# Two recurrent attention layers and two FFNs on one core: the first and last weight loads in other pieces, and another written order

## The chip, the cores and the metric

One core of one Trainium2 chip. The metric is device time in microseconds, here the median of five runs. The engines are named as the profile names them: PE is TensorE (PEld its weight loads), DVE is VectorE, ACT is ScalarE, POOL is GpSimd, and SP is SyncE, which only issues DMAs. Each engine, SP too, takes its instructions strictly in program order; an instruction waits for semaphores of other engines or of landed DMAs.

## The reference

The input x is 2048 x 576 in bf16. Block A, a layer of attention with recurrent memory, is applied to layernorm(x) and added to x; block B, a gated FFN, is applied to the layernorm of that and added; then A and B once more, with the same weights.

Block A cuts the sequence into 64 segments of 32 rows. The output of a segment's first 8 rows is the memory of the next one:

```python
for s in range(n_seg):
    xs = x[:, s * seg_len:(s + 1) * seg_len, :].copy()
    h = jnp.concatenate([mem, xs], axis=1)          # 8 + 32 rows
    q = jnp.einsum('btd,dhe->bhte', h, Wq)          # 32 heads of 128; k and v alike
    scores = jnp.einsum('bhqe,bhke->bhqk', q, k) * scale
    scores = jnp.where(mask[None, None], scores, -1000000000.0)
    p = _softmax(scores, axis=-1)
    o = jnp.einsum('bhqk,bhke->bhqe', p, v)
    o = jnp.einsum('bhte,hed->btd', o, Wo)
    mem = o[:, :M, :].copy()
```

Block B is `einsum(silu(x w1) * (x w3), w2)` with a hidden width of 4608.

## The kernel before

**Steps.** The two attention layers run interleaved. Layer two is LAG = 8 segments behind layer one, so there are 72 steps; steps 8 to 63 treat one segment of each layer side by side (80 columns instead of 40), the first and last eight only one. Wq and Wk stay in SBUF in `W` (128 partitions x 9 x 4096: four chunks of 128 input rows for each of Wq and Wk, and the ninth for the remaining 64 rows, Wq's on partitions 0 to 63, Wk's on 64 to 127), Wv in `WV`, Wo in `WO`. The FFN weights do not fit beside them and are streamed again for each block of 128 rows, in 18 tiles ("prs") of 256 hidden columns, through two slots of `W13` (w1 and w3) and two of `W2C` (w2).

**Work of a step, and its letters.** PE's order is written out as a string with one letter for a group of matmuls: Q, eight units of query and key projections of four heads (32 matmuls), and q, their remainder over the last 64 rows (8); S the scores of eight heads; T the transposes of the softmaxed P; P the product with V; O and o the output projection and its remaining 64 columns; V, X, G and v, x, g the value projections and their remainders; F and f the FFN's up projections and remainder, W and w its down projection for layer one and two; m, a, b, p, n transposes around the layernorms. `plan` (line 76) walks PE's letters in the written order and gives the work of the other engines to ACT or DVE by priorities and modelled times; DMA issues go into SP's queue in the order in which the planner comes to them. What matters for PE besides the order is the tiling of its array, `mode` in `make_nodes`: "full" (128 x 128) for Q, T, P, O, F, W, G and the transposes; "row" (two tiles of 64 rows) for q, f, g; "col" (tiles of 64 columns) for S, o and wide V and X; "c32", "oct" and "quad" for the narrow V and X and their remainders.

**What sets the order.** A step begins with Q, which needs the memory rows that the step before wrote from its o (`y_mem`). Scores go over PSUM to DVE (mask add, maximum, subtraction), ACT (exp), DVE (sum, reciprocal, multiplication into `PB`), back to PE (T). All groups take their PSUM from eight banks; a bank is free when its last reader is done. The string is FIRST (16 steps), eleven times FOUR (4 steps), LAST (12 steps).

**First loads** (`load_qk`, line 642; `load_tail`, 649; `load_v`; `load_o`). The order on SP is one half of the remainders, Wq in four transfers of 1 MB, Wk likewise, WV in four, WO in eight pieces of four heads; ACT issues the other half of the remainders. Each unit of Q in step 0 waits for all of Wq and Wk (`ld_qk`). Ahead of the first Q stand 18 matmuls that compute nothing, six for each of three Wk chunks, each waiting for its chunk (`qk`, line 895). At most eight of these transfers are in flight: an issue waits for the one eight places before it.

**Last loads** (`job`, from line 464; `tail_load`, 694). The FFN of the last 128 rows runs when attention is over. Its first two tiles (pr 16 and 17) are kept in W13 and W2C from the FFN before; they are called the kept pair. The other 16 come in eight units of two tiles: units 0, 1 and most of 2 go into `WV`, the rest into `W`, whose space is free when all of the last step's Q are done. They are issued from SP.

**Heads.** Group g of eight heads holds heads 4g to 4g+3 and 16+4g to 16+4g+3 (`head`), and the blocks of `V` and the columns of WV are numbered to match.

Of the kernel before, what the change touches and what calls it, by code (L numbers as in the profile page):

```python
# [13 lines left out]
P = 128  # L14
R64 = 64
D = 576
# [168 lines left out]
def ewh(*ns):  # L185
# [4 lines left out]
FIRST = (  # L190
    "amQqqQSQqQqQQSqqqqQQSSxXVvTPTPOTOPooTOoPOoQQqqvqqSVQQQqSTQqqqQSQPXSxOTPTOPTOPoooOoQQqqqQqSQqSVqvQQqqSQQaTSPTOPTo"
    "PTOPOOoooVqqvQQQSqqQQqqSQQqSqTPQOTSPXoTOPToxPOOooQQpqqqQvSVqqQQnQSfqFQSqqQTFPfSTOFPfWTOPfFToOPFOoooWQqfqQQqfqSFv"
    "VQQSfqFQFqTfSPQqTWPQFffqOTSoxPOWXTFPOFOoooWQfqqQFSfqqQQvVqSTQFqfQQFPfSqqQWOoSTFPfFTOPWTOPooffOoFQQqqVSvWqQFQfqQS"
    "qTWQqqqQPSQTOPabOSXTXPTOPoooxOoxVvpQQqqqQQqnSSqqfQFQfFTSQqqfFPQOTSoWPFTffOPFTOPWOoooFQqqfQQQSqqfFGQqgqQTSSPQgqqO"
    "WGTQFPSofgGTFfGPOTgfFPOWOoooFQqfqQWFSqfqQQFqqfSQWQTvVQSfqFPQTqfOSPFTOPfWOTFPFOooooWQfqqQqqfSFQQWQaqqSQQbTQSqgqGS"
    "gPGTGPOTggGPOTOPoooOoQqqppQQQSqqqQnnvVSfqFQFTQPSqfqQFfSWTOPwFTffFPOTOPwOWffooooFQFqqQWwQQSqqQfqFFTSfgqQGwWFPfSQQ"
    "gqqGTGSgPOWTOPwfgGTFPOFOooooffFQQqqvVSqqQQWQqSwTQPFqqQTSffqFQwPOWTSffOPFFTOaPWwOooooFqfqQQWQSqqqQQSQbqqqQQTGgSgS"
    "PGTGPOTggGPOTwPOOoooo"
)
FOUR = (  # L200
    "QqqvpQQpQqqVnSSqQnQFfqfFTQqqSQPFffSTFOPwTWOPFTOPWOfooooFwQqqfQQqqSWQQqqgSQwTGFPSffFGQqgqQTOPFTSfggGGPOTOPWwOoooo"
    "FfqfFQwWFQqfqQQqfvVSSFFQfqqQWTawPFqfqSQQTWOwffoSFPFTOPwTOPWOoooFfqqQQWQqqSQQqqSbQQqqgGTQPSSgGTGPOggTGPOTwPOOoooo"
)
LAST = (
    "VvqqpQQpQqqSQQnSqQnQqqqQTFPSSffTFPOOwFToffPFTOWPFOoooffFQQqqqQWwQSfqqFQWGgqTQSPwFQfqFQTSqfgGGPOTSogOPWwFfgfFTGOP"
    "wWFOfoooFfqqQQWVSqqvQQwFTSfqQFPWwqfQFSqqfQQTwWPSOTFPFffTOPOOooooWQqqQQqqSvQQQqqSVSTQqqbPQTOPvSVXTwPOTOPxoooOoVpp"
    "vqQQqqQQSqnQnQSqqfFQFTqSfqPQOTFPSoffTOFPwTOPWOoooFQqqfQwWFfSvVqqQQFqfqQQWTwSSqQPQFffqFTwOPSWTFffFPOTOPWwOxooooXQ"
    "FqqfQQqfSVvFFfqQWwSFTQfqqQQPSqqTOPQOooSfTWwPFTFPOOooWQfqqQwSqqQQFSqqfQQvVTSWPOTQPQqqwSoTbOoXPTxPOOooQqqqpQQSvqqV"
    "QQnQSfqFSqTQfqPFQTOPSfFwOTFPToofPOOooFQfqqQQSqfqFvVQQQqqSTwPQSqfqQFOSoTFPwTOPfxXTFPOOooowQqfqQQSqfFqVvQQSqqQTQSq"
    "qfFPQOTSofPFOTwPFTOPooffOoFQQqqwSqqQQvqSVqQQwQSTqfFPqQTfSPFTOOPwTOPoooOfopFFnffFwFfffFFwFffwFFfFwffFFwffFFwffFFw"  # L210
    "ffFFwffFFfww"
)
# [10 lines left out]
def make_nodes(em, nseg, pools, o=Opt, dma_bw=230e3, load_bw=400e3):  # L223
# [4 lines left out]
    def node(*a, **k):  # L228
        n = Node(*a, **k)
        nodes.append(n)  # L230
        return n
# [18 lines left out]
    ld_m0 = node("ACT", 0.1, em.load_m0(), prio=-90, name="m0", lat=2.5)  # L250
    ld_t = [node("ACT", 0.2, em.load_tail(1), prio=-80, name="ldt", lat=8.0), load("ldt", kb(R64, 6144), -20, em.load_tail(0))]
    ld_qk = [load("ldqk", kb(512, 4096), kind - 9.0, em.load_qk(kind)) for kind in (0, 1)] + ld_t
    ld_v = [load("ldv", kb(512, 4096), -7.0, em.load_v())] + ld_t
    ld_o = [load("ldo", kb(1024, 576), g - 6.0, em.load_o(g)) for g in range(NG)]
# [45 lines left out]
    def v_nodes(name, t, k, prio, tail_at, emit, strips, deps, tail_deps, free):  # L300

        modes = ("col", "quad") if strips[0][3] == R64 else ("c32", "oct")
        b = banks()
        m_ = node("PE", 8 * 0.2158, emit(b, False), deps=deps, prio=prio, mode=modes[0], acq=b, name=name)
        n = node("PE", 0.2158, emit(b, True), deps=deps + tail_deps, prio=prio + tail_at, mode=modes[1], acq=b, name=name + "t")
        reads_ht.setdefault(t, []).extend([m_, n])
        for r in (0, 1):
            outs = em.v_parts(strips, r)
            b[r].users = len(outs)
            for p0, width, row, blk in outs:  # L310
                e = node("AD", ew(512), em.v_ev(b[r], p0, width, row, blk), deps=[m_, n] + free.get(blk % 4, []), prio=prio + 0.01 * (blk % 4),
                         rel=[b[r]], name=name + "e")
                vx_ev.setdefault((name, t, blk % 4), []).append(e)
        return [m_, n]
# [16 lines left out]
    def vg_out(t, g, b, deps, row):  # L331

        return [node("AD", ew(512), em.v_ev(b[r], row, R64, row, NG * r + g), deps=deps, prio=t + o.vm + 0.01 * g + (0.05 if row == 0 else 0.0), rel=[b[r]],
                     name="VGe") for r in (0, 1)]
# [10 lines left out]
    def step(t):  # L345
# [17 lines left out]
        for g in range(NG):  # L363
            qs, qe = [], []
            for u in (2 * g, 2 * g + 1):
                q = Slot("qkt", users=1)
                b = banks()
                pq = t + o.qk + o.ustep * u
                m_ = node("PE", 32 * mm80, em.qk(t, u, b), deps=hx + hm[:1] + (ld_qk if t == 0 else []),
                          prio=pq, mode="full", acq=[q] + b, name="QK")  # L370
                n = node("PE", 4 * mm80, em.qk_tail(t, u, b), deps=hx + hm + (ld_qk if t == 0 else []), prio=pq + o.qkt, mode="row",
                         acq=[q] + b, name="QKt")
# [72 lines left out]
    def job(j):  # L445
# [18 lines left out]
        if last:  # L464
            v_done, qk_done, wo_done = last_reads
            tail = []
            for i in range(8):
                if i == 2:
                    parts = [(0, 9 * 512, v_done), (1, 4 * 576, qk_done)]
                else:  # L470
                    parts = [(None, 9 * 512 + 4 * 576, v_done if i < 2 else qk_done + wo_done[max(i - 4, 0):i - 3])]
                tail.append([load("tail", kb(128, c), s0 + o.tail_at + 0.01 * i, em.tail_load(i, what), deps=dep) for what, c, dep in parts])
# [89 lines left out]
class Emitter:  # L562
# [78 lines left out]

    def load_qk(self, kind):
        def f(n):
            wd = (self.a.wq, self.a.wk)[kind]
            for c in range(4):
                self.dma(self.T.W[:, 4 * kind + c, :], wd[c * P:(c + 1) * P, :])
        return f

    def load_tail(self, r):

        def f(n):
            go, wd, rr = ((self.dma, self.a.wq), (self.adma, self.a.wk))[r] + (slice(r * R64, (r + 1) * R64),)
            go(self.T.W[rr, 8, :], wd[4 * P:D, :])
            go(self.wv(True)[rr, :], self.a.wv[4 * P:D, r * 2048:(r + 1) * 2048])
        return f
# [6 lines left out]
    def load_v(self):  # L662
        def f(n):
            for c in range(4):
                self.dma(self.wv(False)[:, c, :], self.a.wv[c * P:(c + 1) * P, :])
        return f

    def load_o(self, g):
        def f(n):
            for h0 in (4 * g, H // 2 + 4 * g):  # L670
                self.dma(self.T.WO[:, h0:h0 + 4, :], self.a.wo[h0:h0 + 4].rearrange("h e d -> e h d"))
        return f

# [20 lines left out]
    def tail_load(self, i, what):  # L694

        def f(n):
            T = self.T
            qk, wv = T.W[:].rearrange("p a b -> p (a b)"), T.WV[:]
            n13, n2 = 9 * 512, 4 * D
            k = n13 + n2  # L700
            if i < 2:
                t13, t2 = wv[:, i * k:i * k + n13], wv[:, i * k + n13:(i + 1) * k]
            elif i == 2:
                t13, t2 = wv[:, 2 * k:2 * k + n13], qk[:, 5 * k:5 * k + n2]
            else:
                t13, t2 = qk[:, (i - 3) * k:(i - 3) * k + n13], qk[:, (i - 3) * k + n13:(i - 2) * k]
            fa = i * 512
            t13 = t13.rearrange("p (c f) -> p c f", c=9)
            t2 = t2.rearrange("p (b d) -> p b d", b=4)
            if what != 1:  # L710
# [105 lines left out]
    def v_mm(self, t, b, strips, tail):  # L816
# [4 lines left out]
        for c in ((4,) if tail else range(4)):  # L821
            for r in (0, 1):
                for p0, c0, q, m, row in strips:
# [4 lines left out]
                    else:  # L828
                        w0 = (4 * r + q) * 512
                        self.mm(out, HTt[:, c, c0:c0 + m], W[:, c, w0:w0 + 512], first and c == 0, c == 3, tile_position=(0, p0))  # L830

    def vg(self, t, g, b, tail):

        def f(n):
# [4 lines left out]
            for c in ((4,) if tail else range(4)):  # L839
                for r in (0, 1):  # L840
# [3 lines left out]
                    else:  # L844
                        w0 = (4 * r + g) * 512
                        self.mm(self.bk(b[r])[:], HTt[:, c, 32:160], W[:, c, w0:w0 + 512], first and c == 0, c == 3)
# [6 lines left out]
    def narrow(self, c0, row):  # L853

        return [(64 * ab + 32 * i, c0, 2 * i + ab, 32, row) for ab in (0, 1) for i in (0, 1)]

# [8 lines left out]
    def v_parts(self, strips, r):  # L865

        return [(p0, m, row, 4 * r + q) for p0, _, q, m, row in strips]

# [14 lines left out]
    def head(self, g, j):  # L883

        return H // 2 * (j // 4) + 4 * g + j % 4

    def qk(self, t, u, b):

        def f(n):
            q0, q1 = self.qcols(t)  # L890
            HTt = self.ht(t)
            first = self.begin(b)
            for c in range(3 if t == u == 0 else 0):
                for _ in range(6):
                    self.mm(self.bk(b[1])[:], self.T.ident[:, 0:P], self.T.W[:, 4 + c, 0:512], True, True)
            for j in range(4):
# [423 lines left out]
```

## Time and profile before

| | |
|---|---|
| median of 5 runs | 2710.03 us (2707.76 to 2711.33) |
| profiled execution | 2710.07 us, span 2708.3 us, mean granted PE clock 0.997 |
| PE busy | 2646.2 us, 98% |
| DVE, ACT, POOL busy | 78%, 51%, 12% |
| HBM | read 308.49 MB, written 2.36 MB: 115 GB/s over the span |
| DMA queue q1 | 477,696 packets, 38.0% of 16 engines' span |

The page gives busy time by engine, the chain of work that ended last, and groups of instructions with the idle time before them and what ended it. A matmul's mean time is its latency; consecutive ones overlap, and how far apart they start is read from the trace's start times. The window view gives the same busy times for chosen stretches. The waits view names who waited for whom; the timeline gives instructions in order, equal neighbours merged, with start and length.

### The profile page before, as it was taken

Reading aid. Unit: us, or ns where it says so; the run is one execution under the profiler, and the core shown is the slowest. Engines: PE = TensorE matmul, PEld = TensorE weight load, DVE = VectorE, ACT = ScalarE, POOL = GpSimd, SP = SyncE. Lnnn points to the kernel's source line nnn. Section 1 sums busy time; section 2 is a strip of 40 time slices with the busy share of each in tenths; the row PEclk is TensorE's granted clock in tenths of the full one; section 3 lists DMA queues with packets and bytes.
Section 4 is the critical chain, followed back from the end, with each engine's and each line's share of the span. In section 5 each row is a group of like instructions: output and inputs, shape, how many; then the busy total and the mean of one; then the engine's idle time right before and its main releaser. Section 6 shows DMA issues by size and latency. Waiting matters only on the chain.

```text
span 2708.3 us, 126684 instructions
## 1 busy us (share of the span) xinstructions
PE 2646.2 (98%) x55801; PEld 2229.9 (82%) x55801; DVE 2105.5 (78%) x5431; ACT 1378.4 (51%) x3970; POOL 333.3 (12%) x400
## 2 busy tenths in 40 slices
PE   5999999999999999999999999999999999999998
PEld 3788888888888888888888888888888888888886
DVE  4778887887878788787878878787887878787876
ACT  2655554554545455454545545454554545354553
POOL 1111110110101011010101101010110101011110
PEclk8999999999999999999999999999999999999999
DMA  9064533334342433434233343423334342425358
GB/s 315 4 175 129 147 94 114 88 109 125 99 133 79 117 89 109 125 99 131 80 116 92 110 125 96 135 76 116 95 110 125 92 132 70 134 88 151 94 169 260
DMA packets 481593, 321.42 MB, mean 119 GB/s; under 512 B 26280, under 2 KB 476720, under 8 KB 479376
## 3 DMA queue, kind: packets, MB, share of 16 engines
q1 hardware_dynamic: 477696, 305.44, 38.0%
q8 instruction: 437, 7.16, 1.1%
q0 software_dynamic: 3024, 6.93, 0.9%
q10 hardware_dynamic: 320, 0.94, 0.1%
q14 instruction: 116, 0.95, 0.1%
HBM read 308.49 MB, written 2.36 MB: 115 GB/s over the span
## 4 chain that ended last, share of the span: by engine, by line
PE 90%; DVE 4%; DMA 3%; ACT 2%; issue 1%; SPq 0%; POOL 0%; ACTq 0%; DVEq 0%
PE bank L581 90%; DMA W<-in_B_w_dram 1%; DVE STAT L587 1%; ACT V L584 1%; DVE SME L587 1%; DVE HTT L587 1%; DMA W<-in_A_Wk_dram 1%; DVE PB L587 1%; DVE V L587 1%; DMA WV<-in_A_Wv_dram 0%; DMA W2C<-in_B_w_dram 0%; SPq L590 0%; DVE PTS L587 0%; ACT QKT L584 0%; ACT HT L584 0%
## 5 line engine op out<-in xcount | busy, mean ns | idle before, releaser
L581 PEld LDWEIGHTS <-W 128*128 128x128 bf16 (+1 forms) x29400 | 1226.6, 98 | 145.7 <-issue 50.2
L581 PE MATMUL bank<-HT,W 128*128 128x80 bf16 (+3 forms) x23040 | 811.0, 197 | 11.7 <-ACT HT L584 6.2
L581 PE MATMUL bank<-XTB,W 128*128 128x256 bf16 (+3 forms) x6360 | 651.2, 262 | 6.6 <-DMA W<-in_B_w_dram 5.8
L584 ACT ACTIVATE QKT<-bank 128x256 bf16<-128x256 f32 (+4 forms) x1555 | 366.5, 308 | 408.2 <-PE bank L581 394.2
L999 POOL MEMSET PB<- 128x1024 bf16 x288 | 274.1, 952 | 1802.4 <-PE bank L581 1502.2
L581 PE MATMUL bank<-OT,WO 128*128 128x80 bf16 (+2 forms) x11520 | 409.6, 198 | 1.7 <-DVE OT L587 0.7
L584 ACT ACTIVATE V<-bank 64x512 bf16<-64x512 f32 (+1 forms) x605 | 342.9, 587 | 122.6 <-PE bank L581 116.4
L581 PEld LDWEIGHTS <-WO 128*128 128x128 bf16 (+1 forms) x11520 | 380.4, 102 | 17.5 <-issue 8.9
L581 PE MATMUL bank<-WV,HT 128*32 128x512 bf16 (+4 forms) x3240 | 367.1, 383 | 1.9 <-ACT HT L584 1.3
L581 PE MATMUL bank<-W2C,HTT 128*128 128x288 bf16 x2240 | 315.7, 286 | 0.7 <-DMA W2C<-in_B_w_dram 0.6
L587 DVE TENSOR_REDUCE STAT<-SME 104x8 f32<-104x320 f32 (+1 forms) x576 | 275.2, 478 | 16.8 <-ACT SME L584 11.6
L587 DVE TENSOR_TENSOR PB<-SME,STAT 40x128 bf16<-40x128 f32 (+4 forms) x912 | 275.6, 336 | 13.5
L584 ACT ACTIVATE HTT<-bank 128x512 bf16<-128x512 f32 (+1 forms) x324 | 178.1, 550 | 189.6 <-PE bank L581 187.5
L587 DVE SCALAR_TENSOR_TENSOR HTT<-HTT,bank 128x512 bf16<-128x512 bf16 (+1 forms) x324 | 201.1, 621 | 78.4 <-ACT HTT L584 76.8
L581 PEld LDWEIGHTS <-HT 128*32 128x32 bf16 (+4 forms) x3240 | 138.5, 96 | 147.7 <-issue 24.2
L587 DVE SCALAR_TENSOR_TENSOR XR<-bank,XR 128x288 f32<-128x288 f32 x576 | 243.5, 448 | 9.7 <-PE bank L581 3.2
L581 PEld LDWEIGHTS <-HTT 128*128 128x128 bf16 x2304 | 210.0, 98 | 48.2 <-issue 0.8
L587 DVE TENSOR_TENSOR HTT<-HTT,bank 128x512 bf16<-128x512 bf16 (+1 forms) x324 | 203.6, 628 | 30.0 <-DVE HTT L587 1.4
L584 ACT ACTIVATE SME<-SME 104x320 f32<-104x320 f32 (+1 forms) x288 | 136.0, 472 | 175.4 <-DVE SME L587 172.0
L587 DVE CAST QKT<-bank 128x128 bf16<-128x128 f32 (+2 forms) x493 | 136.6, 318 | 107.9 <-PE bank L581 105.0
L584 ACT ACTIVATE OT<-bank 128x320 bf16<-128x320 f32 (+1 forms) x382 | 144.6, 406 | 141.0 <-PE bank L581 137.8
L587 DVE CAST V<-bank 64x512 bf16<-64x512 f32 (+1 forms) x259 | 177.1, 684 | 39.4 <-PE bank L581 34.1
(64 smaller groups left out, 1805.1 us busy)
## 6 DMA issues: line engine op xcount, KB each, us to landing
W<-in_B_w_dram SPq DMA_DIRECT2D x612, 256.0 KB, 3.4
W2C<-in_B_w_dram SPq DMA_DIRECT2D x306, 288.0 KB, 3.1
W<-in_B_w_dram SPq DMA_DIRECT2D x612, 32.0 KB, 3.1
W<-in_B_w_dram SPq DMA_DIRECT2D x10, 512.0 KB, 9.1
WO<-in_A_Wo_dram SPq DMA_DIRECT2D x8, 576.0 KB, 9.2
XR<-in_A_x_dram POOLq DMA_DIRECT2D x16, 288.0 KB, 2.9
W<-in_A_Wq_dram SPq DMA_DIRECT2D x4, 1024.0 KB, 14.8
W<-in_A_Wk_dram SPq DMA_DIRECT2D x4, 1024.0 KB, 17.1
```

The lines of the kernel that those rows point to most:

```text
L581: self.ch("PE", self.nc.tensor.matmul(out, lhsT=lhsT, rhs=rhs, start=start, stop=stop, skip_group_check=True, **k))
L584: self.ch("ACT", self.nc.scalar.activation(*a, **k))
L587: self.ch("DVE", getattr(self.nc.vector, fn_)(*a, **k))
L999: return lambda n: self.ch("POOL", self.nc.gpsimd.memset(self.T.PB[:, pb.i], 0.0))
```

## The change

1. Wq and Wk load by halves of the heads (columns 0 to 2047, then 2048 to 4095): for each half the four chunks of Wq, the four of Wk (512 KB each), then both remainders (256 KB each), all from SP. A unit of Q in step 0 waits only for its own half. WV's two remainders follow WV's four mains, on SP.
2. The groups hold eight consecutive heads, so WO loads in four transfers of eight heads. V's blocks and WV's columns are numbered anew to match.
3. There are 12 warming matmuls, three for each of four Wk chunks.
4. The last FFN's units load otherwise: unit i's w1 and w3 go into the 512 columns of `W` that the last step's Q unit i read, its w2 into `WV`. The first waits for that unit of Q, the second for the last V; units 4 to 7 also for an output projection.
5. FIRST, FOUR and LAST are new strings with the same number of each letter.

```diff
+    ld_h = [load("ldqk", kb(512 + 2 * R64, 4096), half - 9.0, em.load_qk(half)) for half in (0, 1)]
+    ld_v = [load("ldv", kb(512 + 2 * R64, 4096), -7.0, em.load_v())]
-                m_ = node("PE", 32 * mm80, em.qk(t, u, b), deps=hx + hm[:1] + (ld_qk if t == 0 else []),
+                m_ = node("PE", 32 * mm80, em.qk(t, u, b), deps=hx + hm[:1] + ([ld_h[u // 4]] if t == 0 else []),
...
             for i in range(8):
-                if i == 2:
-                    parts = [(0, 9 * 512, v_done), (1, 4 * 576, qk_done)]
-                else:
-                    parts = [(None, 9 * 512 + 4 * 576, v_done if i < 2 else qk_done + wo_done[max(i - 4, 0):i - 3])]
+                late = wo_done[i - 4:i - 3] if i >= 4 else []
+                parts = [(0, 9 * 512, qk_done[2 * i:2 * i + 2] + late), (1, 4 * 576, v_done + late)]
...
+    def load_qk(self, half):
+        def f(n):
+            h = slice(half * 2048, (half + 1) * 2048)
+            for kind, wd in ((0, self.a.wq), (1, self.a.wk)):
+                for c in range(4):
+                    self.dma(self.T.W[:, 4 * kind + c, h], wd[c * P:(c + 1) * P, h])
+            for kind, wd in ((0, self.a.wq), (1, self.a.wk)):
+                self.dma(self.T.W[kind * R64:(kind + 1) * R64, 8, h], wd[4 * P:D, h])
+        return f
...
+            for r in (0, 1):
+                self.dma(self.wv(True)[r * R64:(r + 1) * R64, :].rearrange("p (q n) -> p q n", q=NG),
+                         self.a.wv[4 * P:D, :].rearrange("p (q r n) -> r p q n", q=NG, r=2)[r])
...
-            for h0 in (4 * g, H // 2 + 4 * g):
-                self.dma(self.T.WO[:, h0:h0 + 4, :], self.a.wo[h0:h0 + 4].rearrange("h e d -> e h d"))
+        return lambda n: self.dma(self.T.WO[:, g * GH:(g + 1) * GH, :], self.a.wo[g * GH:(g + 1) * GH].rearrange("h e d -> e h d"))
...
+            t13, t2 = T.W[:, :, fa:fa + 512], T.WV[:, i * 4 * D:(i + 1) * 4 * D].rearrange("p (b d) -> p b d", b=4)
...
-        return H // 2 * (j // 4) + 4 * g + j % 4
+        return GH * g + j
...
-            for c in range(3 if t == u == 0 else 0):
-                for _ in range(6):
-                    self.mm(self.bk(b[1])[:], self.T.ident[:, 0:P], self.T.W[:, 4 + c, 0:512], True, True)
+            for c in range(4 if first and t == 0 and u % 4 == 0 else 0):
+                for _ in range(3):
+                    self.mm(self.bk(b[1])[:], self.T.ident[:, 0:P], self.T.W[:, 4 + c, u * 512:(u + 1) * 512], True, True)
```

FOUR, the part of the order that is repeated, before and after:

```diff
-    "QqqvpQQpQqqVnSSqQnQFfqfFTQqqSQPFffSTFOPwTWOPFTOPWOfooooFwQqqfQQqqSWQQqqgSQwTGFPSffFGQqgqQTOPFTSfggGGPOTOPWwOoooo"
-    "FfqfFQwWFQqfqQQqfvVSSFFQfqqQWTawPFqfqSQQTWOwffoSFPFTOPwTOPWOoooFfqqQQWQqqSQQqqSbQQqqgGTQPSSgGTGPOggTGPOTwPOOoooo"
+    "QqQpQpQqqqvVSSnnQFffqqFQQTFSffqqQPFTWSPOwTFPOTOPwOooooWQQqqqfQSQQQqqqfFGgfSSTFPFQqfqgGQTWwPFTSfggGFPGOTOPOOooooW"
+    "wQQqqqfQFQvfqfVSSwFQWQFqffqFWTQPwTFSffqqQOPWoSwTFPFOTOPwWOoooffFQqqQWQSqqqQaQSbQQTQqqqgGSSgPGTGPOTggGPOTwPOOoooo"
```

## The prediction

> **What bounds the kernel now.** I read the busy times first, then the stages, then what TensorE (PE) waited for, and only then single pieces of the timeline.
>
> ```profile
> PE 2646.2 (98%) x55801; PEld 2229.9 (82%) x55801; DVE 2105.5 (78%) x5431; ACT 1378.4 (51%) x3970; POOL 333.3 (12%) x400
> PE 90%; DVE 4%; DMA 3%; ACT 2%; issue 1%; SPq 0%; POOL 0%; ACTq 0%; DVEq 0%
> ```
>
> PE is busy 98% of the span and is 90% of the chain that ended last. What takes PE's issue time is therefore worth its full time in the middle of the run. The stages (window, length, then PE, PEld, DVE, ACT, POOL busy; granted clock, DMA share, GB/s) show where that does not hold:
>
> ```profile
> 0.00:62.10 62.10, 31.39 (x684) 22.68 (x685) 26.24 (x66) 15.08 (x39) 10.36 (x23) 0.89 0.97 341
> 62.10:532.10 470.00, 459.30 (x11101) 388.63 (x11101) 375.61 (x1018) 249.91 (x746) 65.56 (x75) 1.00 0.37 108
> 532.10:2272.10 1740.00, 1733.73 (x34390) 1461.96 (x34391) 1364.05 (x3476) 904.69 (x2586) 204.19 (x243) 1.00 0.37 107
> 2272.10:2658.50 386.40, 382.13 (x9020) 324.55 (x9020) 310.68 (x800) 198.47 (x574) 51.12 (x58) 1.00 0.44 128
> 2658.50:2708.30 49.80, 39.67 (x614) 32.13 (x612) 28.89 (x72) 10.24 (x27) 2.09 (x3) 0.99 0.88 270
> ```
>
> Step 0 (until 62.1) and the last FFN (from 2658.5) have the DMA at 97% and 88%; between them it is at 37 to 44% and PE hardly stops. The eleven repeats of FOUR are 532.1 to 2272.1, 158.2 us each. PE's waits (total, times, longest):
>
> ```profile
> PE bank L581 <- DMA W<-in_A_Wk_dram: 13.7, 3, 12.5
> PE bank L581 <- DVE XN L587: 10.8, 1, 10.8
> PE bank L581 <- ACT HT L584: 7.5, 19, 0.8
> PE bank L581 <- DMA W<-in_B_w_dram: 5.8, 5, 1.7
> ```
>
> The Wk wait is step 0; of the five waits for FFN weights three, 4.3 of the 5.8 us, lie in the tail. What is left to save in the middle is PE's own order, and there one thing costs issue time without computing: a change of the array's tiling.
>
> ```profile
> 754.52 1.91 PE L581 MATMUL bank<-XTB,W 128*128 128x256 bf16 x16
> 756.27 0.45 PE L581 MATMUL bank<-ident,PB 104*128 104x80 bf16 x8
> ...
> 794.66 1.91 PE L581 MATMUL bank<-XTB,W 128*128 128x256 bf16 x16
> 796.51 0.32 PE L581 MATMUL bank<-HT,W 64*128 64x80 bf16 x8
> ```
>
> The same sixteen FFN matmuls hold PE 1.75 us (754.52 to 756.27) ahead of another full-array group and 1.85 us (794.66 to 796.51) ahead of a two-row-tile group. By the starts of consecutive matmuls between 400 and 2500 us: full to full 36 ns apart at 80 columns, full to row 134, row to full 131; at 256 columns 109 and 205. A switch costs 0.09 to 0.12 us, in either direction.
>
> **The change, part by part.** The sum is made against the profiled execution, 2710.07 us (span 2708.3 and 1.8 around it); the median of the runs shown is 2710.03.
>
> *Order.* Counting changes of mode letter by letter along PE's order: FIRST 352 to 322, FOUR 74 to 65 in each of eleven repeats, LAST 285 to 258; in all 1451 to 1295, 156 fewer. The number of matmuls is otherwise the same, but for 6 fewer warming ones. With each group priced at its median in this trace, with or without a switch behind it, PE's work falls by 14.8 us (95 ns a switch). Of this 1.0 lies in step 0 and 3.0 behind the FFN-down group ahead of the kept pair's (the tail, below), both bound otherwise; 10.8 us lie where PE has no cover: **-10.8**.
>
> *What the new order may make wait.* I set the PE work between each producer and its consumer beside the old order's and looked at what the old gap cost. In FOUR the smallest gaps are alike: projections to memory write to next QK 0.0 us in both (one stall of 0.41 per repeat in the trace, so it stays), P^T eviction to PV 0.98 and 0.98, FFN product to down 2.70 and 2.79, softmax to transpose 5.66 and 5.89. Two are tighter. First, twice per repeat a QK tail takes the bank of scores 0.61 us behind them, when the mask add on DVE (0.486 us mean) must have read it. The old order's tightest bank, 0.59 us behind a PV eviction, never stalled. From below that is 0; from above one PB multiply of three parts (3 x 0.336) still ahead of the add gives 1.0, times 22 is 22 us. I take 0.1, near the lower row since it has the same gap: **+2.2**. Second, W13 slots are read by an FFN tail 5.03 and 4.87 us behind their release (old minimum in FOUR 5.34). In the old FIRST, gaps of 4.91, 4.94 and 5.0 cost nothing, one of 4.64 cost 0.8 and one of 4.93 cost 1.35. Bounds 0 and 1.35 x 11 = 15; at 0.05 each: **+0.6**.
>
> *First weights.* The windows of step 0:
>
> ```profile
> 0.00:14.60 14.60, 0.93 (x10) 0.75 (x11) 8.87 (x20) 2.24 (x5) 5.88 (x18) 1.00 0.89 222
> 14.60:31.70 17.10, 6.31 (x25) 2.43 (x24) 0.00 (x0) 0.00 (x0) 0.00 (x0) 1.00 1.01 422
> 31.70:46.40 14.70, 11.23 (x345) 10.36 (x345) 6.45 (x19) 3.70 (x13) 0.00 (x0) 0.73 1.03 404
> 46.40:62.10 15.70, 12.91 (x307) 9.13 (x305) 10.92 (x29) 9.14 (x21) 4.48 (x5) 0.82 0.96 303
> ```
>
> Now the queries and keys run from 31.7, when all of Wq and Wk has landed, to 46.4; V starts then, though WV landed at 42.9. Afterwards the first half (4.7 MB) lets four of eight units start near 16 us: 4.7/0.42 and 2.3 until data flows give 13.5 to 15, and 12 warming matmuls of 0.43 at the slow clock follow the first layernorm (12.9). The second half lands near 26, these units end near 34, and V waits for WV instead. So V's start, not the QKs', sets the gain: the wait for Wk is replaced by one for WV. SP's queue carries the same bytes ahead of it, and its two WV remainders now stand behind the mains. The four 64-row transfers that opened the old load, with 222 GB/s until 14.6, come later and in between. If that slow start goes, (14.6-2.3) x 0.422 - 3.24 MB = 1.95 MB, or 4.6 us, are won and V starts at 38.5, 7.9 earlier; if those transfers are as slow where they stand now, WV lands at 42.9 and V starts near 43.4, 3 earlier. Best case 37, 9.4 earlier. WO's last quarter is no limit: it landed at 55.0 and was used at 60.8. I take 7, nearer to the first, since the two windows of 128-row transfers both ran over 400 GB/s: **-7.0**. ACT loses two issues (0.56 and 0.61) at a time when it is idle: nothing.
>
> [...]
>
> *Last weights.* W2b is an FFN-down group of the second layer. The tail in the chain of waits (start, length, what):
>
> ```profile
> 2661.49 6.49 DMA W2C<-in_B_w_dram
> 2668.01 9.54 DMA W<-in_B_w_dram
> ...
> 2678.69 9.75 DMA W<-in_B_w_dram
> ```
>
> The bulk of the last 14 MB lands at one unit (1.77 MB) per 5.31 us: the remainders of units 2 and 7 land at 2672.8 and 2699.3. From the end of the W2b ahead of the kept pair (2658.5) to the start of the very last one (2702.7) it takes 44.2 us. In the new program SP takes the W13 parts of units 0 and 1 during the last step, but units 2 to 7 (30 issues) stand behind the kept pair's two W2C loads, and these wait for that same W2b. So the loads do not follow the last step unit by unit: SP, which takes its queue in order, holds six of eight. From the W2b's end, W2C and unit 2's W13 part, 1.77 MB from an idle queue, need 7.5 us (2 to land, 5.3 at that rate, the issue), five more units 26.6: unit 7 has landed after 34.1. Four FFN-up groups and one W2b (3.1) then make 37.2 instead of 44.2: **-7.0**. PE alone would need 33.9 (31.7, and 2.2 of warming matmuls), so SP's order costs 3.3 here. The kept pair's W2C has 3.4 us to land, at a median of 3.1, and a stall of it is hidden in the wait for unit 7. The loads for the last ordinary FFN tiles, queued behind units 0 and 1, have 5.2 to 7.5 us. POOL's queue issues none of the moved loads.
>
> Head order, V blocks, one WO transfer for two: the same instructions on other addresses: 0.
>
> **Sum.** 2710.07 - 10.8 + 2.2 + 0.6 - 7.0 - 7.0 = 2688.1; I say **2688**.
>
> **Rivals.**
> 1. *The loads give little, the order all.* The 64-row transfers stay slow (start -3), and units 0 and 1, taken early, delay ordinary W13 loads, so that 5 of the tail's 7 are lost. 2710.1 - 10.8 + 2.8 - 3 - 2 = **2697**. For it: 222 GB/s. Against it: in the tail the order of bytes, not their number, changes.
> 2. *Slower: DVE's queue holds the score banks.* If the mask add stands behind an FFN product pair (0.679 + 0.688) and part of a multiply, each of the 22 places costs 1.6 us, 35 in all: 2710.1 - 24.8 + 35 = **2720**. It decides from (24.8 + 5.4)/22 = 1.37 us a place. For it: DVE is 78% busy. Against it: PE's longest wait for DVE behind step 0 is 0.8 us, and in DVE's new order a PB multiply or a residual add precedes the mask add, not a product.
> 3. *The same mechanism at 1.0 us a place:* 2710.1 - 24.8 + 22 = **2707**, no difference.
> 4. *Everything goes through:* V at 37 (-9.4), no new stall, and the tail bound by PE: -10.8 - 9.4 - 10.3 gives **2680**.
>
> **How the numbers follow.** Forecast 0.60, rival 1 0.17, rival 4 0.15, rival 3 0.04, rival 2 0.04. The range 2679 to 2699 takes rivals 1 and 4 in, and the bounds of the start (3 to 9.4) and of a 0.5 us stall at the 22 places. About 0.2%, 5.4 us, is what a measurement tells from no change here: faster 0.92, same 0.04, slower 0.04.
>
> **What would show it.** FOUR's repeat falls from 158.2 to near 157.6, with stalls of PE on DVE at the QK tails if I am wrong there. The first QK starts near 16 us, V near 39, and PE's wait for Wk gives way to waits for Wk's second half and for WV. At the end PE still waits 3 to 4 us in all for units 4 to 7, and SP issues unit 2 only behind the W2b. A repeat above 158.2, or V after 43, would make the prediction wrong.

## The result and the profile after

The changed kernel takes 2701.45 us (median of 21 runs, 2697.20 to 2706.71); before, measured beside it, takes 2709.98 (41 runs). The ratio is 0.9969, 95% interval 0.9963 to 0.9975: 8.5 us faster, where 22 were forecast. The profiled execution took 2704.18 us (span 2702.3), so the two traces differ by 6.0 us, and that difference is what the stages below add up to.

From the page after: the busy line of PE, and the chain of work that ended last, by engine.

```profile
PE 2641.3 (98%) x55795; PEld 2227.8 (82%) x55795; DVE 2089.6 (77%) x5376; ACT 1369.3 (51%) x4025; POOL 333.6 (12%) x400
PE 88%; ACT 4%; DMA 3%; DVE 3%; issue 1%; SPq 1%; POOL 0%; DVEq 0%; ACTq 0%; POOLq 0%
```

PE is as full as before. The stages (window, length, then PE, PEld, DVE, ACT, POOL busy; granted clock, DMA share, GB/s): step 0, the eleven FOURs, the rest of LAST, and the end.

```profile
0.00:60.20 60.20, 32.11 (x680) 22.09 (x681) 27.92 (x68) 14.22 (x39) 10.35 (x23) 0.80 0.99 337
528.70:2262.90 1734.20, 1726.87 (x34387) 1458.78 (x34387) 1359.13 (x3454) 888.00 (x2608) 204.26 (x243) 1.00 0.37 108
2262.90:2655.00 392.10, 385.32 (x9085) 326.48 (x9085) 304.65 (x783) 202.79 (x595) 52.27 (x59) 1.00 0.44 129
2655.00:2702.30 47.30, 37.78 (x550) 31.02 (x547) 28.22 (x70) 9.96 (x25) 1.14 (x2) 0.96 0.84 261
```

Step 0 still moves 337 GB/s at a DMA share of 99%, as before (341): the same bytes, no faster. And what PE waited for (total, times, longest):

```profile
PE bank L578 <- DMA W<-in_A_Wq_dram: 10.7, 1, 10.7
PE bank L578 <- DMA W<-in_B_w_dram: 6.0, 7, 2.4
PE bank L578 <- issue: 4.6, 4, 2.1
PE bank L578 <- DMA WV<-in_A_Wv_dram: 2.3, 3, 0.9
```

The wait for Wk has become a wait for the second half's remainder and for WV, as forecast; but the FFN's weights are waited for as long as before (6.0 against 5.8), in the tail 3.9 against 4.3. Each stage's forecast is the prediction's sum, cut at the same places. PE's work is what the groups take at before's medians, with the tiling switches of each order; the tail begins at the FFN-down group (W2b) ahead of the kept pair's.

| stage | forecast | before | after | change | of it PE's work |
|---|---|---|---|---|---|
| start to first Q of step 1 | -7.0 | 62.36 | 60.16 | -2.2 | -1.0 |
| to the first FOUR | -2.4 | 469.70 | 468.58 | -1.1 | -2.4 |
| eleven FOURs | -6.3 | 1740.03 | 1734.15 | -5.9 | -9.1 |
| LAST up to that W2b | +0.7 | 385.45 | 391.12 | +5.7 | +0.7 |
| that W2b to the very last one | -7.0 | 45.13 | 42.69 | -2.4 | -3.0 |

The eleven FOURs came as forecast. The 16 us that are missing were expected at the start (4.8), in LAST (5.0) and in the tail (4.6), with 1.3 between step 1 and FOUR.

### The profile page after: what moved, and what is told of

Read it like the earlier page. It is cut to its first block, busy times and chain, and to the rows that moved or that the text cites. A ratio compares the mean times of both kernels' runs of the same rounds, so it can differ in the third digit from the quotient of the medians.

```text
span 2702.3 us, 126634 instructions
## 1 busy us (share of the span) xinstructions
PE 2641.3 (98%) x55795; PEld 2227.8 (82%) x55795; DVE 2089.6 (77%) x5376; ACT 1369.3 (51%) x4025; POOL 333.6 (12%) x400
## 3 DMA queue, kind: packets, MB, share of 16 engines
q8 instruction: 437, 7.16, 1.1%
## 4 chain that ended last, share of the span: by engine, by line
PE 88%; ACT 4%; DMA 3%; DVE 3%; issue 1%; SPq 1%; POOL 0%; DVEq 0%; ACTq 0%; POOLq 0%
PE bank L578 88%; ACT V L581 3%; DMA W<-in_B_w_dram 2%; DVE SME L584 1%; DMA W<-in_A_Wk_dram 1%; SPq L587 1%; DMA WV<-in_A_Wv_dram 1%; DVE STAT L584 1%; DVE V L584 0%; ACT SME L581 0%; ACT XTB L581 0%; ACT PTS L581 0%; ACT QKT L581 0%; DVE OT L584 0%; DMA XN<-in_A_x_dram 0%
## 5 line engine op out<-in xcount | busy, mean ns | idle before, releaser
L578 PE MATMUL bank<-XTB,W 128*128 128x256 bf16 (+3 forms) x6480 | 662.5, 261 | 6.9 <-DMA W<-in_B_w_dram 6.0
L581 ACT ACTIVATE QKT<-bank 128x256 bf16<-128x256 f32 (+3 forms) x1587 | 366.6, 317 | 369.7 <-PE bank L578 351.1
L578 PE MATMUL bank<-OT,WO 128*128 128x80 bf16 (+3 forms) x11520 | 406.7, 198 | 0.6 <-DVE OT L584 0.3
L584 DVE CAST QKT<-bank 128x192 bf16<-128x192 f32 (+2 forms) x461 | 125.0, 317 | 137.2 <-PE bank L578 135.9
L581 ACT ACTIVATE PTS<-bank 128x320 bf16<-128x320 f32 (+1 forms) x385 | 144.7, 403 | 162.5 <-PE bank L578 125.8
```

The costliest lines, as they stand in the source:

```text
L578: self.ch("PE", self.nc.tensor.matmul(out, lhsT=lhsT, rhs=rhs, start=start, stop=stop, skip_group_check=True, **k))
L581: self.ch("ACT", self.nc.scalar.activation(*a, **k))
L584: self.ch("DVE", getattr(self.nc.vector, fn_)(*a, **k))
```

## The experiments

All were timed in the same manner, each group of four beside runs of before on its own chip; so ratios are compared, not medians. The changed kernel's is 0.9969.

### Order and loads apart

**Order alone.** The three strings of the changed kernel in the kernel before (named here for which kernel they are from).

```diff
-ORDER = OLD_FIRST + OLD_FOUR * 11 + OLD_LAST
+ORDER = NEW_FIRST + NEW_FOUR * 11 + NEW_LAST
```

> The new order strings on the old loads, first and last. Theory A, read from the two traces: the order gives nearly all of the gain and the loads, together, next to nothing; then this kernel takes about 2701 us, as the changed one does. Theory B, the prediction's steps: order -10.8, its new waits +2.8, so 2702, and the loads' 14 us were lost to something that the loads themselves brought. Theory C: the new order brings the half-clock stretches of TensorE and the late stalls, and the loads give what is gained; then 2706 or more. A and B differ in the next kernels, C falls or stands here.

Measured: 0.9974 (0.9964 to 0.9985), 7.0 us faster.

**Loads alone.** The changed kernel with the three old strings.

```diff
-ORDER = NEW_FIRST + NEW_FOUR * 11 + NEW_LAST
+ORDER = OLD_FIRST + OLD_FOUR * 11 + OLD_LAST
```

> The old order strings on the new loads, first and last (and 12 more warming matmuls, since the old strings begin unit 4 with its full-array part). Theory A: within 3 us of before, about 2709. Theory B (loads worth -14 when no new order disturbs them): 2696. Theory C: about 2703.

Measured: 1.0009 (1.0001 to 1.0018), 2.4 us slower. In its step 0 the value projections stood 7.8 us for WV's remainders, which the old order uses first and the new loads bring last; the first Q of step 1 came at 63.9.

**Old last loads, all else new** (`tail_load` is put back with it).

```diff
-                late = wo_done[i - 4:i - 3] if i >= 4 else []
-                parts = [(0, 9 * 512, qk_done[2 * i:2 * i + 2] + late), (1, 4 * 576, v_done + late)]
+                if i == 2:
+                    parts = [(0, 9 * 512, v_done), (1, 4 * 576, qk_done)]
+                else:
+                    parts = [(None, 9 * 512 + 4 * 576, v_done if i < 2 else qk_done + wo_done[max(i - 4, 0):i - 3])]
```

> New order, new first loads, old last loads (each unit's place and waits as before). The profiled tail of the changed kernel ran from the end of the FFN-down group to the last one in 41.8 us where before had 44.2, but the stretch of the last steps ahead of it took 5.0 us more than its PE work explains before. Theory A: the early units cost about what the shorter tail gives, so this takes 2700 to 2703. If the early units are a net loss: 2697 to 2699, and PE's waits in the last steps without a releaser (instructions not there) fall from 3.2 us to about 1. If the last loads were a gain by themselves: 2704 to 2708.

Measured: 0.9968 (0.9956 to 0.9979).

**Old first loads, all else new** (with the old V blocks and columns of WV).

```diff
-    ld_h = [load("ldqk", kb(512 + 2 * R64, 4096), half - 9.0, em.load_qk(half)) for half in (0, 1)]
+    ld_qk = [load("ldqk", kb(512, 4096), kind - 9.0, em.load_qk(kind)) for kind in (0, 1)] + ld_t
...
-        return GH * g + j
+        return H // 2 * (j // 4) + 4 * g + j % 4
```

> New order, old first loads (and the old order of heads and V blocks that go with them), new last loads. The first QK of step 1 started 2.2 us earlier in the changed kernel. Theory A: without the new first loads 2702 to 2705, with that QK back near 62 us. If the new first loads cost more than they give (half-clock stretches of TensorE between 98 and 231 us come from the shifted start): 2697 to 2700.

Measured: 0.9973 (0.9962 to 0.9983), the first Q of step 1 at 63.2.

What follows from the four: theory A stands. The order gives 7.0 of the 8.5 us; the first loads give 1 us or nothing (0.9973 against 0.9969), the last loads nothing (0.9968 against 0.9969), and both without the new order cost 2.4. Theories B and C fall.

One number more is in their traces. LAST and tail together took 430.6 us in before, 433.8 in the changed kernel, 432.2 with the order alone, 433.8 with the loads alone, 431.5 with old last loads and 430.8 with old first loads, though the new order has 2.3 us less work there. Order and loads move this stretch by 3 us at most, and not by what they save. With the new order and the old last loads PE stands ahead of the W2b, before an ordinary FFN tile whose W13 SP had issued behind unit 0 (from the trace of the order alone):

```profile
2652.01 0.40 PE L581 MATMUL bank<-XTB,W 128*128 128x128 bf16 x4 [3.91 <-DMA W<-in_B_w_dram]
```

That tile waits 4.5 us there and 3.5 with old last loads; in the changed kernel all such waits of LAST are 0.5, but its tail is longer (42.7 against 39.7 and 38.1). What one place saves, the other pays.

### The start: what a 64-row transfer costs

In the changed kernel the 512 KB transfers of 128 rows landed 1.27 us apart; around the 64-row ones the distance was 2.1 to 4.3 us. The windows show it (columns as above):

```profile
14.00:17.00 3.00, 3.00 (x36) 1.38 (x35) 0.00 (x0) 0.00 (x0) 0.00 (x0) 1.00 1.01 239
17.00:26.00 9.00, 3.94 (x146) 3.55 (x142) 3.62 (x10) 1.84 (x6) 0.00 (x0) 0.82 1.02 406
26.00:30.40 4.40, 0.00 (x0) 0.00 (x0) 0.00 (x0) 0.00 (x0) 0.00 (x0) 0.50 1.05 282
38.80:46.40 7.60, 4.89 (x67) 2.27 (x68) 4.26 (x13) 1.91 (x5) 0.00 (x0) 0.78 1.07 262
```

With the three pairs of 64-row transfers in flight (the first, third and fourth line) the DMA engines are as busy as in the second line, but move 239 to 282 GB/s instead of 406. In the trace's packets, one of 4 KB takes 159 ns in the 128-row transfers (median) and mostly 270 to 300 in the 64-row ones. Two runs ask whether it is the rows.

**The remainders on ACT's queue**, beside SP's mains:

```diff
-                self.dma(self.T.W[kind * R64:(kind + 1) * R64, 8, h], wd[4 * P:D, h])
+                self.adma(self.T.W[kind * R64:(kind + 1) * R64, 8, h], wd[4 * P:D, h])
...
-                self.dma(self.wv(True)[r * R64:(r + 1) * R64, :].rearrange("p (q n) -> p q n", q=NG),
+                self.adma(self.wv(True)[r * R64:(r + 1) * R64, :].rearrange("p (q n) -> p q n", q=NG),
```

> The changed kernel with the six 64-row transfers of the start (remainders of Wq, Wk and WV) issued from ACT's queue, beside SP's 128-row ones instead of between them. In the changed kernel the 512 KB transfers of 128 rows land 1.27 us apart, but 2.1 to 4.3 us pass around each pair of 64-row ones, 7.7 us in all. Theory 64-row: such a transfer leaves part of the DMA idle while it stands alone; beside others it costs only its bytes. Then WV's mains land near 38 (39.8 to 44.0 now), the first QK of step 1 starts near 57 (60.2 now), the whole takes 2697 to 2699. Rival, bytes: the DMA is bound by bytes or by row length (2 to 4 KB pieces) whatever the queue; then that QK stays at 59 to 61 and the time within 1.5 us of the changed kernel's.

Measured: 0.9960 (0.9948 to 0.9972). In its trace, the slowest of its runs, WV's last main landed at 44.7 and the first Q of step 1 started at 58.6: 1.6 us of the 3 expected, between what the two theories gave. The remainders cost nearly as much beside other transfers as between them.

**The same bytes in 128 rows:**

```diff
-            for kind, wd in ((0, self.a.wq), (1, self.a.wk)):
-                self.dma(self.T.W[kind * R64:(kind + 1) * R64, 8, h], wd[4 * P:D, h])
+            self.dma(self.T.W[:, 8, h], self.a.wq[3 * P:4 * P, h])
...
-            for r in (0, 1):
-                self.dma(self.wv(True)[r * R64:(r + 1) * R64, :].rearrange("p (q n) -> p q n", q=NG),
-                         self.a.wv[4 * P:D, :].rearrange("p (q r n) -> r p q n", q=NG, r=2)[r])
+            self.dma(self.wv(True)[:, :].rearrange("p (q n) -> p q n", q=NG),
+                     self.a.wv[3 * P:4 * P, :].rearrange("p (q r n) -> r p q n", q=NG, r=2)[0])
```

> The changed kernel with the pairs of 64-row transfers of the start replaced by one transfer of 128 rows with the same bytes each (the remainder rows of Wq, Wk and WV so hold other rows of those matrices, and the output is not the reference's). In the changed kernel's trace a 4 KB packet takes 159 ns in the 128-row transfers and 304 ns in the 64-row ones, with the DMA engines busy all the time. Theory rows: a transfer to 64 partitions costs about twice the DMA time for its bytes wherever it stands, 1.5 MB at 213 instead of 420 GB/s, 3.6 us; then WV has landed by 43 (46.4 now), the first QK of step 1 starts at 56.5 to 58 (60.2 now), and the whole is 2 to 3.5 us below the changed kernel. Rival: the DMA is as slow with these bytes in 128 rows (its place in the queue or its short pieces cost the time); then WV lands at 45.5 to 46.5 and nothing changes.

Measured: 0.9951 (0.9939 to 0.9963), 4.9 us below the changed kernel by the ratios. The same windows of its trace:

```profile
14.00:17.00 3.00, 3.00 (x45) 1.63 (x45) 0.00 (x0) 0.00 (x0) 0.00 (x0) 1.00 1.02 408
26.00:30.40 4.40, 1.60 (x53) 1.56 (x54) 0.00 (x0) 0.01 (x1) 0.00 (x0) 0.50 1.04 427
38.80:46.40 7.60, 4.60 (x84) 2.03 (x77) 6.53 (x12) 5.87 (x12) 0.95 (x1) 0.95 1.08 386
```

The slow windows are gone: all of WV landed at 40.2 (46.4 in the changed kernel), V started at 36.8 (40.4), and the first Q of step 1 at 54.4 (60.2), though PE now stood 1.4 us for WO. The edit also halves the number of these transfers; but between 14 and 17 us the median 4 KB packet took 160 ns here and 273 in the changed kernel, so it is the transfer itself that runs faster. So the price of the 64-row transfers is shown, 5.8 us at that place; it was estimated at 3.6 beforehand. Why such a transfer runs slower, no run shows. The kernel before seems to have paid for it too: its 8 KB packets took a median 502 ns from 2.3 to 14.6 us, and 314 from there to 31.7.

### The end: which bytes stand behind which wait

SP's issues in the changed kernel, from its timeline (start, length, queue, what, how many):

```profile
2646.09 1.05 SPq L587 DMA_DIRECT2D W2C<-in_B_w_dram  x2
2649.66 2.13 SPq L587 DMA_DIRECT2D W<-in_B_w_dram  x4
2651.83 1.14 SPq L587 DMA_DIRECT2D WV<-in_B_w_dram  x2
2654.93 0.88 SPq L587 DMA_DIRECT2D W2C<-in_B_w_dram  x2
```

SP stands from 2647.1 to 2649.7 before an ordinary W13 load whose slot is not free, and from 2653.0 to 2654.9 before the kept pair's W2C loads. By 2647.5 the last V and all of the last step's Q were done, so the space of every unit was free. Meanwhile the DMA was idle four tenths of the time:

```profile
2642.00:2655.00 13.00, 12.82 (x325) 11.87 (x323) 9.69 (x26) 9.23 (x27) 3.81 (x4) 0.91 0.60 172
2655.00:2692.00 37.00, 31.77 (x495) 26.12 (x492) 25.07 (x62) 8.51 (x22) 1.14 (x2) 1.00 1.05 329
```

**Four parts of units 0 to 2, 2.9 MB, moved forward in SP's order**, nothing else:

```diff
+    for ns, ref in (([units[0][1], units[1][1]], w13s[-2]), ([units[2][0]], w13s[-1]), ([units[2][1]], w2ls[-2])):
+        for n in ns:
+            order.remove(n)
+        at = order.index(ref)
+        order[at:at] = ns
```

Here `units[i]` holds the W13 and the W2 part of unit i, `w13s` and `w2ls` the ordinary loads in their order.

> The changed kernel with three units' last loads moved forward in SP's order: W2 of units 0 and 1 ahead of the last W13 load but one, W13 of unit 2 ahead of the last ordinary W13 load, W2 of unit 2 ahead of the kept pair's W2C loads. Units 3 to 7 stay behind these. Their places in W and WV are free from 2647 us at the latest, and the DMA runs at 114 to 268 GB/s from 2644 to 2654. Theory queue order: the end is set by the time at which SP can start the bulk; about 1.2 MB more is moved before 2655, so unit 7 lands and the kernel ends 3 to 4 us earlier (2697 to 2698). Rival: the earlier loads are paid back by late ordinary W13 and W2C loads and by late instructions of PE in the last step; then 2700 to 2703.

Measured: 0.9958 (0.9946 to 0.9970), 2.9 us below the changed kernel by the ratios, at the edge of what was expected; the intervals still overlap. In the trace PE no longer waits for any unit's weights (3.9 us in the changed kernel); 1.0 us of waits for an ordinary W13 stand ahead of the W2b and one of 1.3 us marked "issue" stands behind it. The tail fell from 42.7 to 37.7, LAST and tail together from 433.8 to 427.9.

**W13 of unit 3 as well:** the last list is `[units[2][1], units[3][0]]`.

> As the kernel before it, and W13 of unit 3 also ahead of the kept pair's W2C loads: 1.2 MB more. Theory queue order: 4 to 6 us earlier than the changed kernel (2695 to 2697), less up to 1 us for the kept pair's W2C landing near 2662.6 where W2b wants it at 2662.0. Rival: 2700 or more, with PE's waits for W2C or for ordinary W13 above 3 us in the last 50 us.

Measured: 0.9963 (0.9951 to 0.9975): no further gain. With the four parts alone no wait for units was left to save. From 2600 us on, the trace (of a run 3.4 us above the median) has none either, and instead:

```profile
PE bank L579 <- issue: 7.0, 5, 2.4
PE bank L579 <- DMA W2C<-in_B_w_dram: 0.8, 2, 0.4
```

**Units 0 and 1 moved back** behind the last ordinary W13 load:

```diff
+    for ns, ref in (([units[0][0], units[0][1], units[1][0], units[1][1]], w2ls[-2]),):
```

> The changed kernel with W13 of units 0 and 1 moved back behind the last ordinary W13 load, so that no last weights are loaded before 2650 us. In the other kernels PE's waits that no engine or load explains end 1.1 to 1.7 us behind a 16 KB packet of PE's instruction queue. Theory fetch: PE's instructions come late while weights are loaded at 300 GB/s and more; without the early units these waits between 2600 and 2650 fall from 3.2 us to 1 or less and the FFN-down group ahead of the kept pair starts 2 to 3.5 us earlier; but 2.4 MB more has to be moved behind it, so the end is 2 to 5 us later than in the changed kernel (2704 to 2707). If early units are a net loss: 2698 to 2700. Rival to fetch: these waits stay where they were.

Measured: 0.9991 (0.9983 to 1.0000), 6.0 us above the changed kernel. LAST up to the W2b took 390.0 (391.1 in the changed kernel), the tail 49.1 (42.7), with 4.8 us of waits for W2C. The waits marked "issue" between 2600 and 2650 fell from 3.2 to 1.7, and one of 1.4 us stayed: half of them at most was due to the early units.

So the early units are no net loss: without them the kernel is 6 us slower, 4.8 of it in waits for the kept pair's W2C, ahead of which SP now puts them. The expected gain ahead of the W2b, 2 to 3.5 us, came to 1.1. What sets the end is how many bytes SP has got out before it stops at an ordinary load, and how full the DMA is from 2642 us on.

### What "issue" is

In these lines (changed kernel, then the kernel with unit 3 moved) PE stops in the middle of a group, with nothing that it waits for:

```profile
2633.30 0.99 PE L578 MATMUL bank<-HT,W 128*128 128x40 bf16 x33 [1.09 <-issue]
2640.05 1.69 PE L578 MATMUL bank<-WV,HT 128*32 128x512 bf16 x21 [2.07 <-issue]
```

```profile
2638.91 0.99 PE L579 MATMUL bank<-HT,W 128*128 128x40 bf16 x33 [1.50 <-issue]
2645.12 1.38 PE L579 MATMUL bank<-WV,HT 128*32 128x512 bf16 x21 [1.52 <-issue]
2662.53 0.65 PE L579 MATMUL bank<-OT,WO 128*64 128x40 bf16 x29 [2.40 <-issue]
```

The page has a DMA queue for instructions, q8: 437 packets, 7.16 MB, 1.1% of the 16 DMA engines' span. Its packets follow PE's work: the eleven FOURs have 269 of them and 34,387 matmuls, 128 to a packet, so I take the queue for PE's. PE runs 55,795 matmuls and as many weight loads; if the queue brings these alone, 7.16 MB over 111,590 is 64 bytes for each, and 128 matmuls with their loads in a packet of 16 KB, an estimate from these counts. In the traces of before, the changed kernel, the order alone and the 128-row start, each of the 20 such waits ended 1.2 to 1.6 us after the end of such a packet: 2630.95 to 2631.91 before 2633.30, 2637.48 to 2638.64 before 2640.05. So I infer that PE waited for its instructions; no run changed these packets alone. In the steps with one layer a matmul of 40 columns starts every 25 ns, so 16 KB last 3.2 us at best, an estimate; in FOUR a packet comes every 6.4 us (269 in 1734). How much of the waits is due to the weights' transfers is not shown: with the early units moved back, half of them stayed. No theory of the prediction had this.

### The clock

**Fillers where PE waited:** 14 matmuls with thrown-away results in four groups of the changed kernel.

```diff
+            for _ in range(2 if (t, g) in ((2, 1), (7, 0)) else 0):
+                self.mm(self.bk(b[1])[:], self.T.ident[:, 0:P], self.T.WO[:, 0, 0:512], True, True)
...
+            k = 4 if ents == [(0, 0)] and pr == 5 and tail else 6 if last and pr == 14 and tail else 0
+            for _ in range(k if first else 0):
+                self.mm(self.bk(b[1])[:], self.T.ident[:, 0:P], self.T.WO[:, 0, 0:512], True, True)
```

> The changed kernel with 14 dense filler matmuls (128x512, results thrown away) where PE waited just before a half-clock stretch: two ahead of a PV group of step 2, four ahead of an FFN tail in step 4, two ahead of a PV group of step 7, six ahead of an FFN tail that waits for unit 7. Theory clock: where what PE streams in one 3.41 us stretch, weighed by the share of the array that it uses, falls below about 1.2 us, the next stretch runs at half clock; so the stretches at 156.0, 227.6 and 2692.1 are gone, one or both at 97.9 too, the mean clock rises from 0.992 to 0.994 to 0.995, and the time falls by 1 to 3 us (0.9 us a stretch by the spread of the runs, less up to 1 us of fillers that don't fit into the wait). Rival: the stretches come from something else than what PE streams; then they stay, and the time rises by 0.5 to 3 us.

Measured: 0.9958 (0.9945 to 0.9971), 3.0 us below the changed kernel with overlapping intervals, with a mean clock over its runs of 0.9944 (changed kernel 0.9933, before 0.9967). Windows of the changed kernel, and the same of this one; the column behind POOL is the granted clock:

```profile
152.60:156.00 3.40, 1.92 (x79) 1.70 (x77) 0.88 (x3) 0.15 (x1) 0.00 (x0) 0.99 0.93 241
156.00:159.40 3.40, 3.40 (x78) 2.23 (x74) 2.24 (x6) 0.80 (x3) 0.00 (x0) 0.50 0.65 205
```

```profile
156.00:159.40 3.40, 3.40 (x98) 2.21 (x101) 1.86 (x6) 0.80 (x3) 0.00 (x0) 1.00 0.63 168
```

The stretches at 156.0, 227.6 and 2692.1 are gone, the one at 97.9 is not (96.6), and others are there at 79.6 and 2632.7. The kernel with the four moved parts has none of the first three either, without fillers; so a single trace doesn't show the cause.

A count over traces shows the condition, though not by an edit that sets it. The granted clock changes on a grid of 3.413 us: behind the first 60 us the changed kernel's half-clock stretches are 3.413 us long, one is 6.827, and one the end cuts off. For each stretch at full clock I added up what PE streamed in it: its columns at 2.4 a ns (matmuls of 256 columns started 109 ns apart, of 512 216, so 107 ns for 256 more), times the share of the array's rows and columns in use. In the ten traces with complete records, after some 60 us, a stretch below 1.1 us was followed by half clock in 23 of 23 cases, one of 1.1 to 1.3 in 8 of 14, one above 1.3 in none of some 7600. PE's plain busy time does not separate them: half clock followed a stretch with 2.9 us of it, full clock one with 1.9. So in these traces half clock came also behind stretches in which PE was busy most of the time, but streamed about a third of the 3.4 us or less. By an estimate from these numbers 40-column matmuls come to that (17 ns of streaming every 25 ns) with 1.6 us of waits in the stretch, or with fewer where groups on half the array stand among them.

What it costs is not settled. Between runs of one kernel the time falls by 1.26 us (standard error 0.20) per 0.001 of mean clock, over 151 runs; by that the changed kernel's 0.0034 is worth 4.3 us, part of it in step 0, where PE waits anyway. But a kernel with fillers beside one without, below, differs by nothing.

### Together

**Remainders on ACT's queue and the four parts moved forward:**

```diff
-                self.dma(self.T.W[kind * R64:(kind + 1) * R64, 8, h], wd[4 * P:D, h])
+                self.adma(self.T.W[kind * R64:(kind + 1) * R64, 8, h], wd[4 * P:D, h])
...
+    for ns, ref in (([units[0][1], units[1][1]], w13s[-2]), ([units[2][0]], w13s[-1]), ([units[2][1]], w2ls[-2])):
```

> 64-row transfers of the start on ACT's queue together with the earlier places in SP's queue for W2 of units 0 to 2 and W13 of unit 2. Alone these gave 2.4 and 2.9 us beyond the changed kernel by their ratios to before, each about as large as its uncertainty. If both are real and independent: ratio 0.995 (13.5 us below before). If they are noise or share one limit: 0.996 to 0.997.

Measured: 0.9949 (0.9937 to 0.9961), 2697.34 beside 2710.76, the whole sum of both: 13.8 us faster than before and 5.4 below the changed kernel, with intervals that no longer touch. Its end, to be set beside the two windows of the changed kernel above:

```profile
2642.00:2652.30 10.30, 9.99 (x297) 9.40 (x295) 7.99 (x23) 7.76 (x24) 3.35 (x4) 1.00 1.01 316
```

316 GB/s instead of 172 ahead of the kept pair's W2C; LAST and tail together take 428.1 us instead of 433.8.

**The same with the 14 fillers** (the edit shown above).

> The kernel before it with the 14 filler matmuls of the clock experiment. Theory clock: 1 to 2 us below it at a mean clock higher by 0.001 or so. Rival: the same, or 0.5 to 1 us above, since the other stretches start elsewhere in each run.

Measured: 0.9948 (0.9937 to 0.9960), mean clock 0.9944 (0.9938 without). No difference.

## Why the prediction was right and wrong

The direction was right (faster, given 0.92), the size was not: 2688 with 2679 to 2699 against 2701.45. Rival 1, "the loads give little, the order all", is nearest to what happened, beyond its own 2697. Its first reason holds, the 64-row transfers stayed slow; its second, late ordinary W13 loads, cost only 0.5 us in LAST.

**Order, -10.8: right in kind, 7.0 with its waits against 8.0.** An undisturbed FOUR fell from 158.17 to 157.49 (157.6 forecast); four of the eleven were 0.13 to 0.34 us longer and one 0.88, by single small stalls. With the order alone, step 1 to FOUR took 2.9 us less, FOUR 5.3, and the end gained nothing.

**What the new order may make wait, +2.2 and +0.6: near in sum, by luck: place and engine were wrong.** In the FOURs 3.2 us came of the 2.8 (-5.9 in time against -9.1 of work). But neither of the two QK tails close behind scores stalls: in the ninth repeat one such group of scores starts at 1810.14, the tail at 1810.95 with no idle time. Another QK tail stalls, once per repeat, 0.36 us beyond its pace (4.0 in all): by the planner's bank numbers it takes banks of V, and it waits for V's evictions on ACT, not for DVE's mask add. From the changed kernel's timeline, the second half of that tail:

```profile
1803.72 0.30 PE L578 MATMUL bank<-HT,W 64*128 64x80 bf16 x7 [0.19 <-ACT V L581]
```

Rivals 2 and 3, which had DVE hold the banks of scores, fall. Since the old order's smaller stalls went, an undisturbed repeat stands 1.10 us in all where it stood 0.95. Two waits at FFN tails, 0.3 and 0.4, are W13's margins; all that the repeats took beyond 157.49 each is 1.8 us.

**First weights, -7.0: the step "V's start, not the QKs', sets the gain" failed.** The value projections did start 6.1 us earlier (46.41 to 40.35), but then stood for WV's last main and remainders, which landed at 46.4, after 42.9 in before; the first Q of step 1 gained 2.2 us. From the changed kernel's timeline:

```profile
40.35 2.75 PE L578 MATMUL bank<-WV,HT 128*32 128x512 bf16 x24
44.03 0.62 PE L578 MATMUL bank<-WV,HT 128*32 128x512 bf16 x8 [0.93 <-DMA WV<-in_A_Wv_dram]
46.41 4.09 PE L578 MATMUL bank<-WV,HT 64*32 64x512 bf16 x44 [0.65 <-DMA WV<-in_A_Wv_dram]
```

The assumption beneath it was that the slow start "goes" with the remainders' place in the queue. The other bound had them "as slow where they stand now", with WV at 42.9 and 3 us won, and even that was too kind: they were slow in all three places. The second half landed at 32.5 instead of near 26, so that the queries and keys ended near 40 instead of 34, and WV landed 3.5 us later than in before, when V needed it. The choice between the bounds was made by the 128-row windows over 400 GB/s, which said nothing of 64-row transfers; the only row that did was the 222 GB/s until 14.6. The 128-row run shows what was missed.

**Last weights, -7.0: the step "W2C and unit 2's W13 part, 1.77 MB from an idle queue, need 7.5 us" failed first.** The queue was not idle: W2 of units 0 and 1, 1.2 MB, had been issued at 2651.8, and unit 2's W13 landed 9.2 us after the W2b, unit 7's 37.0 after it (34.1 forecast). Behind that came 4.7 us instead of 3.1, in a half-clock stretch from 2692.1. But the larger error was to price the tail from the W2b alone. The stretch ahead of it, priced at +0.7, grew by 5.7: 2.1 of it are waits marked "issue" (3.2 against 1.1), and a half-clock stretch at 2640.9 lies in it; some 2 us in small waits I cannot assign, and their cause stays open. Reading SP's head-of-line wait as the thing that holds six of eight units was right, as moving parts ahead of it showed; that before had the same six units behind the same wait, so that the change did not touch it, should have been seen in the old trace.

**The size that has no step:** the clock between step 1 and FOUR (two half-clock stretches by 105 us, two more by 231) and the waits marked "issue" in LAST; both lie outside what the prediction looked at.

**Halves:** 512 KB transfers landed 1.27 us apart and 1 MB ones 2.5, so halves cost nothing by themselves; the prediction's sum has no term for them.

## What to carry to other kernels

Price a load by the partitions that it reaches as well as by its bytes: 1.5 MB in transfers of 64 rows took 5.8 us more than in 128 rows here. Before a load is said to be earlier, write down SP's order with what each issue waits for, in the old trace as in the new: the rearranged last loads, six of eight units behind the same wait as before, gave nothing here (0.9969 with them, 0.9968 without), and the 2.9 MB that were moved ahead of it gave 2.9 us by the ratios. PE was 98% busy here, and yet stood 4.6 us in waits marked "issue" and had a mean clock of 0.9933 where before had 0.9967: where nothing is named as releaser, look at the instruction queue's packets and at the granted clock.

## What the runs showed of the hardware

- While pairs of transfers to 64 partitions were in flight, the DMA moved 239 to 282 GB/s, with those to 128 alone 406, at the same DMA share of 100%; 4 KB packets took mostly 270 to 300 instead of 159 ns.
- The 16 KB packets of one instruction queue (437, 7.16 MB) followed PE's work, one for 128 matmuls in the FOURs. While matmuls had 40 columns and weights loaded (272 and 274 GB/s while PE stood in the changed kernel's two waits shown), PE stood for 0.2 to 2.4 us at a time with nothing named that it waited for, and went on 1.2 to 1.6 us after such a packet's end. In FOUR, at 108 GB/s and 80 columns, the four traces have no such wait; the one with old first loads has one, of 0.3 us.
- In ten traces, behind their first 60 us, the granted clock followed what PE streamed in the 3.4 us before, weighed by the array in use: half clock came after all 23 stretches below 1.1 us of streaming, about a third of 3.4, after 8 of 14 from 1.1 to 1.3, and after none of some 7600 above.
